# Running the last head pair with both query halves per key tile, and its batch's dispatch as one group

## The chip, the cores and the metric

The kernel runs on one core of a Trainium2 chip. The metric is device time in microseconds for one execution, lower is better. Engine names in the rows: PE is TensorE, PEld its weight loads, DVE VectorE, ACT ScalarE, POOL GpSimd, SPq the SyncE queue from which all bulk transfers are issued.

## The reference

Three blocks follow one another. First, attention with pooled queries: 4 batches, 8 heads, 1152 keys, head size 64; neighbouring queries are averaged, so there are 576 per head.

```python
q_pool = q.reshape(B, H, S // 2, 2, D).mean(axis=3)
scores = scale * np.matmul(q_pool, k.transpose(0, 1, 3, 2))
attn = softmax(scores)                      # over the 1152 keys
x = np.matmul(attn, v)                      # to (2304 tokens, 512)
```

Second, a soft mixture of 8 experts with 4 slots each (32 slots). The dispatch weights are a softmax over all 2304 tokens, so no slot input is complete before the last token is; the combine weights are a softmax over the 32 slots.

```python
logits = x @ phi                            # 2304 x 32
d = softmax(logits, axis=0); slot_input = d.T @ x
h = np.maximum(slot_input[e] @ w1[e], 0); slot_out[e] = h @ w2[e]   # per expert
c = softmax(logits, axis=1); x = c @ slot_out
```

Third, RMS norm and a gated feed-forward block with inner width 1536, which gives the output.

## The kernel before, in words

**Attention.** Heads are taken two at a time, in 16 pairs, four to a batch. Within a pair there are 9 key tiles of 128 keys and two query halves of 288 queries (`HQ`). `qk` (L421) makes the scores of one key tile and one half with eight matmuls into a two-bank PSUM tile `sc`, and ScalarE turns them into `e` (L423). `add_e` adds up the `e` tiles for the softmax sums (L438; `acc`), in two runs, key tiles 0 to 4 and 5 to 8. `av` multiplies `e` by the values (L444; four matmul instructions per key tile and half).

Pairs 1 to 14 take both halves at each key tile (9 steps, lists `STEP` and `STEP_V`); after every third key tile they do the `av` of the three. Pairs 0 and 15 are in `HALVED`: all 9 key tiles of half 0, then all 9 of half 1 (18 steps, `STEP_0`). In these two pairs VectorE shares the `acc` additions with GpSimd.

**Work beside the key loop.** `side(p)` lists what is done within pair p and when, from tables of due times (`AT`, and for some pairs `AT_0`, `AT_01`, `AT_15`); one unit of due time is one key tile of both halves. It holds the preparation of later pairs, the end of the pair before (copy of the result `take_x`, `sum_up`, `sums`, `recips`, transposes `x_turn`, division `x_divide`, logits `x_logits`, `logit_mul`, `logit_add`), and the dispatch of a finished batch (`d_turn`, `d_exp`, `d_back`, `slot_part`, `slot_turn`). Order on every engine is the order written; engines run in order.

**The last pair.** Its own end can't be put beside a next pair. In the kernel before, half 0 of pair 15 is finished while half 1 runs (the entries ending in `_a`), and batch 3 is dispatched in two groups of 288 tokens: group 3 (half 0) within the pair, group 4 (half 1) after it. `x_logits_last` makes the logits of these tokens with the tokens as the stationary side, so tokens lie on partitions, and `d_turn` turns them back with six small matmuls a group (L563). After the loop come, on the way to the slot inputs `sT`: `take_x`, `recips`, `x_logits_last(1)`, `d_turn(4)`, the exponential, `d_back`, `slot_part(4)`, `slot_copy`, and the join of the groups by the running maximum; then the first expert matmul (`hin`, L1021).

**Weights and buffers.** Each expert takes 4 MB of `w1` and `w2`, 33.6 MB for eight, and 8.4 MB of converted feed-forward weights (`away`) follow. All is loaded in this order through SyncE's queue by `load(n)`, which issues only while the program's own count of free buffers (tags `W`, `A`, `B`, `C`) allows it; at run time an issue waits until the earlier user of its buffer is done, and everything behind it on the queue waits too. `xts`, the two tiles with a batch's normalized tokens, occupy tag `W`, which is worth six units of 256 KB. In the kernel before, one is given back after group 3's `slot_part` and one after group 4's.

Of the kernel before, what the change touches and what calls it, by code (L numbers as in the profile page):

```python
# [18 lines left out]
NP = 16  # L19
# [88 lines left out]
    take_x=0.24,  # L108
    sum_up=[0.25, 0.26],
    sums=0.8,  # L110
    recips=1.33,
    inverse=[1.4, 2.41],
    x_turn=[2.3, 3.3],
    x_divide=[2.4, 3.6],
    x_logits=4.2,
    drop_x=4.25,
    logit_mul=4.8,
    logit_add=4.81,
    take_x_a=5.49,
    sums_a=5.1,  # L120
    recips_a=5.48,
    x_turn_a=[5.8, 6.1],
    x_divide_a=[5.9, 6.2],
    x_logits_a=6.15,
    d_exp_a=7.18,
    d_back_a=7.62,
    slot_part_a=8.2,
    slot_turn_a=9.43,
)
MAX_0 = [2, 1, 1, 1, 1, 0, 1, 1, 1, 1, 1, 1, 1, 1, 1, 1, 0, 0]  # L130
HALVED = (0, 15)
# [30 lines left out]
def attention_softmoe_gated_kernel(ctx: ExitStack, tc: tile.TileContext, kT, qT, vv, ip, cst, w1, w2, wg, wv, wo, rg, out):  # L162
# [311 lines left out]
    def recips(p, hs=(0, 1)):  # L474
        n = len(hs)
        q = slice(64 * hs[0], 64 * hs[-1] + 64)
        o = bank([TB, 3, 64 * n], "sumt")
        for t in range(3):
            pe.transpose(out=o[:, t, :], in_=srow[p][q, TB * t:TB * t + TB], identity=ident[q, q])
        if p == NP - 1:  # L480
            rel("B")
        if p not in rr:
            rr[p] = S([TB, 2, 3, 2], "rr")
        dv.reciprocal(rr[p][:, hs[0]:hs[-1] + 1], o.rearrange("p t (h s x) -> p h t s x", s=2, h=n)[:, :, :, :, 0])
# [52 lines left out]
    def x_logits_last(h):  # L537

        o = bank([TB, 3, 2, 32], "xl")
        if "ls" not in xl:  # L540
            xl["ls"] = S([TB, 3, 2, 2, 32], "ls", tag="lg")
        for t in range(3):
            j = 3 * h + t
            pe.matmul(o[:, t].rearrange("p s l -> p (s l)"), lhsT=xu[NP - 1][:, TB * j:TB * j + TB], rhs=ipt[:, (NP - 1) % 4, :], start=True, stop=True)
        dv.tensor_tensor(out=xl["ls"][:, :, :, h], in0=o, in1=rr[NP - 1][:, h, :, :, None].to_broadcast([TB, 3, 2, 32]), op=ALU.mult)


    dtx, dnx, psb = {}, {}, {}
    groups = [(b, (0, 1)) for b in range(3)] + [(3, (0,)), (3, (1,))]

    def d_turn(g):

        b, hs = groups[g]
        mm = S([32, 2], "mm")
        both = two_banks("lgt") if attention[0] else None
        o = []
        for i, h in enumerate(hs):
            o.append(both[0:32, i, 0:HQ] if attention[0] else bank([32, HQ], "lgt"))
            r = slice(64 * h, 64 * h + 64)
            pe.matmul(o[i], lhsT=stack[r, 0:32], rhs=lg[b][r], start=True, stop=(b < 3))  # L560
            for t in range(3 if b == 3 else 0):
                for s in range(2):
                    pe.matmul(o[i][:, TB * t:TB * t + TB], lhsT=xl["ls"][:, t, s, h], rhs=ident[0:TB, 0:TB], start=False, stop=(s == 1 and t == 2))  # L563
        if len(hs) > 1:
            dv.reduce_max(out=mm, in_=both[0:32, :, 0:HQ], axis=AX.X)
            dv.reduce_max(out=mall[:, g:g + 1], in_=mm, axis=AX.X)
        else:
            dv.reduce_max(out=mall[:, g:g + 1], in_=o[0], axis=AX.X)
        return o
# [8 lines left out]
    def d_exp(g, o, nm):  # L578
        n = len(o)
        dtx[g] = B([32, 576], F32, "dtx")  # L580
        sm = S([32, 2], "sm")
        for h in range(n):
            ac.activation(dtx[g][:, HQ * h:HQ * h + HQ], o[h], AF.Exp, bias=nm, accum_out=sm[:, h:h + 1] if n > 1 else sall[:, g:g + 1])
        if n > 1:
            dv.tensor_tensor(out=sall[:, g:g + 1], in0=sm[:, 0:1], in1=sm[:, 1:2], op=ALU.add)

    def d_back(g):
        n = 3 * len(groups[g][1])
        o = bank([TB, n, 32], "dn")
        for j in range(n):  # L590
            pe.transpose(out=o[:, j, :], in_=dtx[g][:, TB * j:TB * j + TB], identity=ident[0:32, 0:32])
# [3 lines left out]
    def d_copy(g):  # L595
        o = dpart.pop(g)
        dnx[g] = S([TB, 3 * len(groups[g][1]), 32], "dn", bufs=1, tag="ct")
        ac.copy(dnx[g], o)

    def slot_part(g):  # L600
        n, j0 = 3 * len(groups[g][1]), 3 * groups[g][1][0]
        w = 128 if n > 3 else 96
        o = bank([w, 512], "pp")
        last = n - 4 if n > 4 else 0
        for j in reversed(range(n)):
            x = xts[(j0 + j) // 3][:, (j0 + j) % 3].rearrange("p h d -> p (h d)")
            for i in range(2 if j < last else 1):
                q, c = (32 * (j + 2 * i), slice(256 * i, 256 * i + 256)) if j < last else (32 * (j % 4), slice(0, 512))
                pe.matmul(o[q:q + 32, c], lhsT=dnx[g][:, j, :], rhs=x[:, c], start=(j >= last), stop=(j < last or not last))
        dpart[g] = o, w  # L610

    def slot_copy(g, weight=None):
        o, w = dpart.pop(g)
        psb[g] = B([w, 512], F32, "psb")
        if weight is None:
            ac.copy(psb[g], o)
            if g == 3:
                rel("W")
        else:
            by = weight()  # L620
            rel("W")
# [4 lines left out]
    def slot_turn(g, to):  # L626

        w = 128 if len(groups[g][1]) > 1 else 96
        o = bank([128, 4, w], "pto")
        for k in range(4):  # L630
            pe.transpose(out=o[:, k, :], in_=psb[g][:, 128 * k:128 * k + 128], identity=ident[0:w, 0:w])
# [12 lines left out]
    def c_turn(b):  # L644
        o = bank([TB, 3, 64], "lgt")
        for t in range(3):
            pe.matmul(o[:, t], lhsT=lg[b][:, TB * t:TB * t + TB], rhs=pair.rearrange("p h l -> p (h l)"), start=True, stop=(b < 3))
            for s in range(2 if b == 3 else 0):
                pe.matmul(o[:, t], lhsT=ident[0:TB, 0:TB], rhs=xl["ls"][:, t, s].rearrange("p h l -> p (h l)"), start=False, stop=(s == 1))
# [115 lines left out]
    def side(p):  # L765
# [27 lines left out]
        if l >= 0:  # L793
# [4 lines left out]
            at("x_turn", lambda i: x_turn(l, range(3 * i, 3 * i + 3)) if p == NP - 1 else x_turn_all(l))  # L798
# [50 lines left out]
    with tc.manual_schedule():  # L849
# [64 lines left out]
        for p in range(NP):  # L914
# [3 lines left out]
            for u, (kt, h) in enumerate(steps):  # L918
# [4 lines left out]
                for i, step in enumerate(order):  # L923
# [22 lines left out]
        take_x(l, (1,))  # L946
# [3 lines left out]
        recips(l, (1,))  # L950
        load(40)
        gm = S([32, 1], "gm")
        dv.reduce_max(out=gm, in_=mall[:, 0:4], axis=AX.X)
        x_logits_last(1)
        z = bank([TB, 3, 128], "xo")
        for i in range(3):
            pe.transpose(out=z[:, i, :], in_=xu[l][:, HQ + TB * i:HQ + TB * i + TB], identity=ident)
        rel("B")
        r = rr[l][:, 1]
        for i in range(3):  # L960
            for s in range(2):
                c = slice(64 * s, 64 * s + 64)
                if i == 1:
                    dv.tensor_scalar(out=xts[1][:, i, l % 4, c], in0=z[:, i, c], scalar1=r[:, i, s:s + 1], scalar2=None, op0=ALU.mult)
                else:
                    ac.activation(xts[1][:, i, l % 4, c], z[:, i, c], AF.Copy, scale=r[:, i, s:s + 1])
# [382 lines left out]
```

## Time and profile before

| | |
|---|---|
| median of 3 runs | 748.07 us (746.56 to 752.93) |
| the profiled execution | 744.76 us, span of its instructions 742.9 us |
| pair 14 (both halves per key tile) | 424.7 to 450.9 us of the span |
| pair 15 (one half after the other) | 450.9 to 486.8 us |
| after the last `av`, up to the first expert matmul | 486.8 to 497.45 us |
| experts and the rest of the weight stream | 497.45 to about 555 us |
| feed-forward block | about 555 to 742 us |

Busy time of an engine is the union of its instructions; PE's ends are modelled, so its busy share reads high. A row of the chain gives start, duration, engine and line of one link of the work that ended last. A row of the timeline merges like instructions that follow one another on an engine. A row of stretches gives each engine's busy time (with instruction counts), the granted TensorE clock as a share of full speed, the busy share of the DMA engines and the transfer rate.

### The profile page before, as it was taken

To read this page: it belongs to the slowest core of one execution; us is meant where nothing else is said; L and a number is where in the kernel's file an instruction comes from. 1 tells how busy PE (TensorE), PEld (TensorE's weight loads), DVE (VectorE), ACT (ScalarE), POOL (GpSimd) and SP (SyncE) were. 2 spreads that over 40 slices of the span, in tenths; PEclk is the share of its full clock that TensorE was granted. 3 is DMA by queue.
4 is the path that set the end of the run, shared out by engine and by line. 5 is a ranking of instruction groups with operands and counts; after the bars stand their busy time and mean duration, and the time that the engine had idled before them with its cause. 6 is when DMAs were issued, how large, how long until landed. Compare 5 with 4: busy or idle time off the path is not lost.

```text
span 742.9 us, 15218 instructions
## 1 busy us (share of the span) xinstructions
PE 699.8 (94%) x5967; PEld 487.7 (66%) x5967; DVE 478.8 (64%) x691; ACT 391.3 (53%) x809; POOL 422.5 (57%) x340
## 2 busy tenths in 40 slices
PE   4999989899999899999999998989999999999998
PEld 2666656566666566666665665544357888888887
DVE  5968898887787887687897674432053755544420
ACT  2455656566656556565665543432155856554320
POOL 5336877876777677678777665221016854535330
PEclk9999999999999999999999999989999999999999
DMA  5221642844636617427416306079990010000001
GB/s 173 96 88 64 210 153 73 265 134 163 231 123 209 223 59 252 177 67 276 153 44 225 137 11 230 29 258 363 398 401 26 15 44 29 28 30 15 28 29 43
DMA packets 52855, 103.56 MB, mean 139 GB/s; under 512 B 5816, under 2 KB 19632, under 8 KB 52784
## 3 DMA queue, kind: packets, MB, share of 16 engines
q1 hardware_dynamic: 52784, 102.59, 39.6%
q8 instruction: 47, 0.77, 0.4%
q14 instruction: 24, 0.20, 0.1%
HBM read 89.39 MB, written 13.11 MB: 138 GB/s over the span
## 4 chain that ended last, share of the span: by engine, by line
PE 73%; DVE 13%; issue 5%; DMA 4%; ACT 3%; POOL 2%; SPq 0%; ACTq 0%; DVEq 0%; POOLq 0%
PE yo L1252 20%; PE sc L421 16%; PE av L444 15%; DVE mx L365 4%; PE mxp L364 4%; PE gv L1204 3%; DMA w<-away 2%; POOL acc L438 2%; DVE mx L371 2%; ACT e L423 2%; PE sums L469 1%; PE mxp L374 1%; PE hin L1021 1%; PE xl L521 1%; PE xo L504 1%
## 5 line engine op out<-in xcount | busy, mean ns | idle before, releaser
L438 POOL TENSOR_TENSOR acc<-acc,e 128x576 f32<-128x576 f32 x148 | 205.6, 1415 | 59.3 <-ACT e L423 49.9
L423 ACT ACTIVATE e<-sc 128x576 f32<-128x576 f32 x288 | 166.4, 657 | 93.2 <-PE sc L421 90.9
L365 DVE TENSOR_REDUCE mx<-mxp 128x2 f32<-128x1024 f32 x120 | 143.7, 1222 | 55.5 <-PE mxp L364 55.4
L444 PE MATMUL av<-e,vt 128*64 128x288 f32 x1152 | 165.2, 415 | 0.0
L438 POOL TENSOR_TENSOR acc<-e 128x576 f32<-128x576 f32 x60 | 91.9, 1549 | 95.3 <-ACT e L423 88.4
L444 PEld LDWEIGHTS av<-e,vt 128*64 128x64 f32 x1152 | 73.4, 136 | 60.5 <-issue 22.8
L421 PE MATMUL sc<-qh,kh 64*128 64x288 f32 x576 | 97.9, 329 | 3.6 <-DVE xt L513 2.8
L1252 PE MATMUL yo<-woh,hA 128*128 128x512 f32 (+1 forms) x312 | 98.9, 384 | 0.0
L421 PE MATMUL sc<-mr,pick 64*128 64x288 f32 x576 | 88.3, 294 | 1.5 <-DMA mr<-mrow 1.5
L421 PE MATMUL sc<-ql,kh 64*128 64x288 f32 x576 | 87.8, 294 | 0.0
L421 PE MATMUL sc<-qh,kl 64*128 64x288 f32 x576 | 87.7, 294 | 0.0
L1209 DVE SCALAR_TENSOR_TENSOR th<-th,gv 128x384 f32<-128x384 f32 x72 | 39.9, 554 | 62.5 <-ACT th L1206 61.9
L421 PEld LDWEIGHTS sc<-qh,kh 64*128 64x128 f32 x576 | 55.8, 185 | 28.9 <-issue 9.4
L1235 POOL TENSOR_TENSOR hA<-hu,hA 128x384 fp32r<-128x384 f32 x48 | 48.7, 1016 | 43.0 <-ACT hA L1234 39.3
L1252 PEld LDWEIGHTS yo<-woh,hA 128*128 128x128 f32 x312 | 57.6, 188 | 10.2 <-issue 0.7
L421 PEld LDWEIGHTS sc<-mr,pick 64*128 64x128 f32 x576 | 57.2, 187 | 1.9 <-DMA mr<-mrow 1.9
L1252 PE MATMUL yo<-wol,hA 128*128 128x512 f32 (+1 forms) x151 | 57.9, 383 | 0.0
L1206 ACT ACTIVATE th<-gv 128x384 f32<-128x384 f32 x72 | 35.2, 488 | 42.4 <-PE gv L1204 39.1
L421 PEld LDWEIGHTS sc<-qh,kl 64*128 64x128 f32 x576 | 57.1, 189 | 0.2
L421 PEld LDWEIGHTS sc<-ql,kh 64*128 64x128 f32 x576 | 56.9, 187 | 0.0
L364 PE MATMUL mxp<-kh,qh 64*128 64x512 f32 x240 | 49.1, 437 | 0.0
L1211 DVE SCALAR_TENSOR_TENSOR hu<-th,gv 128x384 f32<-128x384 f32 x72 | 39.9, 555 | 8.4 <-DVE th L1209 0.4
(201 smaller groups left out, 1070.9 us busy)
## 6 DMA issues: line engine op xcount, KB each, us to landing
w<-in_w_dram SPq DMA_DIRECT2D x86, 256.0 KB
w<-in_w_dram SPq DMA_DIRECT2D x21, 512.0 KB
vt<-in_vv_dram SPq DMA_DIRECT2D x16, 576.0 KB
qraw<-in_qT_dram SPq DMA_DIRECT2D x15, 576.0 KB
kraw<-in_kT_dram SPq DMA_DIRECT2D x15, 576.0 KB
away<-w SPq DMA_DIRECT2D x32, 256.0 KB
w<-away SPq DMA_DIRECT2D x32, 256.0 KB
raw<-in_wg_dram SPq DMA_DIRECT2D x12, 512.0 KB
```

The costliest lines, as they stand in the source:

```text
L364: pe.matmul(o[:, s, :], lhsT=q[r, 128 * t:128 * t + 128], rhs=k[r, 512 * c:512 * c + 512], start=True, stop=True)
L365: dv.reduce_max(out=heads[:, :, t, c], in_=o, axis=AX.X)
L421: pe.matmul(o[:, s, 0:HQ], lhsT=w[r, wk], rhs=q[r, c], start=(i == 0), stop=(i == 3))
L423: ac.activation(ets[p, kt, h], o[:, :, 0:HQ], AF.Exp, scale=0.0625)
L438: eng.tensor_tensor(out=acc[p, h, j], in0=first[p, h, j] if n == 1 else acc[p, h, j], in1=e, op=ALU.add)
L444: pe.matmul(avt[p, h][64 * s:64 * s + 64, 0:HQ], lhsT=vt[p][:, kt, 64 * s:64 * s + 64], rhs=ets[p, kt, h][:, s], start=(kt == 0), stop=(kt ...
L1204: pe.matmul(o[i], lhsT=sg[n][:, 256 * i + 128 * c:256 * i + 128 * c + 128], rhs=cT[g], start=True, stop=True)
L1206: ac.activation(t, o[0], AF.Tanh, scale=0.5)
L1209: dv.scalar_tensor_tensor(out=t, in0=t, scalar=1.0, in1=o[0], op0=ALU.add, op1=ALU.mult)
L1211: dv.scalar_tensor_tensor(out=u, in0=t, scalar=0.5, in1=o[1], op0=ALU.mult, op1=ALU.mult)
L1235: gp.tensor_tensor(out=b, in0=u, in1=f(a), op=ALU.subtract)
L1252: pe.matmul(o, lhsT=x, rhs=w[:, c], start=(ft == 0 and i == 0), stop=(ft == NF - 1 and i == 2))
```

## The change

Pair 15 leaves `HALVED` and runs like pairs 1 to 14. Pair 14's end is done at the due times of the middle pairs instead of earlier ones. Pair 15's `sums` are due at 8.55, before the last two `av` steps, and are inverted in place. After the loop the whole batch 3 is dispatched as one group of 576 tokens: logits with `ipt` (that is, phi) as the stationary side, four matmuls to bring the two heads' parts together, one exponential over both halves, six transposes back. Both `xts` tiles are given back at the end of `slot_part`. The joining of groups has four instead of five members. The PSUM pool is changed after `sT` instead of before the dispatch.

```diff
 AT_15 = dict(
-    take_x=0.24,
-    sum_up=[0.25, 0.26],
-    sums=0.8,
...
+    x_turn=5.8,
+    x_divide=[5.81, 5.82],
+    drop_x=5.83,
+    sums_a=8.55,
+    inverse_a=[8.56, 8.57],
 )
-HALVED = (0, 15)
+HALVED = (0,)
...
-        eng = dv if p in HALVED and kt % 2 == 0 else gp
+        eng = dv if p in (0, NP - 1) and kt % 2 == 0 else gp
...
+    def d_turn(b, *more):
+        mm = S([32, 2], "mm")
+        both = two_banks("lgt")
+        ins = (lg[b],) + more
+        for n, x in enumerate(ins):
+            for h in range(2):
+                r = slice(64 * h, 64 * h + 64)
+                pe.matmul(both[0:32, h, 0:HQ], lhsT=stack[r, 0:32], rhs=x[r], start=(n == 0), stop=(n == len(ins) - 1))
+        dv.reduce_max(out=mm, in_=both[0:32, :, 0:HQ], axis=AX.X)
+        dv.reduce_max(out=mall[:, b:b + 1], in_=mm, axis=AX.X)
+        return both
...
     def d_exp(g, o, nm):
-        for h in range(n):
-            ac.activation(dtx[g][:, HQ * h:HQ * h + HQ], o[h], AF.Exp, bias=nm, accum_out=sm[:, h:h + 1] if n > 1 else sall[:, g:g + 1])
+        dtx[g] = B([32, 2, HQ], F32, "dtx")
+        ac.activation(dtx[g], o[0:32, :, 0:HQ], AF.Exp, bias=nm, accum_out=sall[:, g:g + 1])
...
         if p == NP - 1:
-            at("take_x_a", lambda i: take_x(p, (0,)))
-            at("x_logits_a", lambda i: x_logits_last(0))
-            at("d_exp_a", lambda i: d_exp(3, d_turn(3), d_neg(3)))
-            at("slot_part_a", lambda i: (slot_part(3), slot_copy(3)))
...
+            at("sums_a", lambda i: sums(p))
+            at("inverse_a", lambda i: inverse(p, i))
...
         l = NP - 1
-        take_x(l, (1,))
-        phase.close()
-        recips(l, (1,))
+        take_x(l)
+        x_logits(l)
+        recips(l)
         load(40)
...
+        dv.tensor_tensor(out=z, in0=xl.pop(l), in1=srow[l], op=ALU.mult)
+        o = d_turn(3, z)
+        x_turn_all(l)
+        r = rr[l]
+        for i in range(3):
+            for s in range(2):
+                c = slice(64 * s, 64 * s + 64)
+                ac.activation(xts[0][:, i, l % 4, c], xo[l, i][0][:, i, c], AF.Copy, scale=r[:, 0, i, s:s + 1])
+        nm = S([32, 1], "nm")
+        dv.tensor_scalar(out=nm, in0=mall[:, 3:4], scalar1=gm, scalar2=-1.0, op0=ALU.max, op1=ALU.mult)
+        x_divide(l, range(3, 6))
+        d_exp(3, o, nm)
...
+        d_back(3)
+        d_copy(3)
...
+        slot_part(3)
+        slot_copy(3, weight)
         keep_b[0] = KEEP[1]
         load(40)
```

## Rows read from the trace of the kernel before

**Rows 1.** Busy time by stretch: us, PE, PEld, DVE, ACT, POOL, clock, DMA, GB/s.
```profile
424.70:450.90 26.20, 25.88 (x269) 18.17 (x267) 17.86 (x26) 12.42 (x24) 18.33 (x14) 1.00 0.23 84
450.90:486.80 35.90, 32.13 (x291) 18.97 (x290) 15.46 (x27) 14.87 (x30) 10.56 (x8) 1.00 0.35 130
486.80:497.45 10.65, 7.47 (x51) 5.00 (x52) 5.56 (x18) 3.75 (x12) 1.26 (x1) 0.86 0.77 272
497.45:510.00 12.55, 11.12 (x121) 5.63 (x122) 3.50 (x9) 3.87 (x9) 4.59 (x6) 0.85 0.91 306
510.00:555.00 45.00, 42.98 (x487) 20.98 (x487) 12.04 (x32) 14.54 (x35) 3.47 (x7) 1.00 1.05 399
555.00:742.00 187.00, 184.89 (x929) 154.62 (x927) 83.53 (x158) 94.49 (x222) 86.88 (x84) 1.00 0.09 33
```

**Rows 2.** Chain of waits, experts' stage: start, us, engine, what.
```profile
530.96 9.02 DMA w<-away
```

**Rows 3.** Chain of waits, last pair and what follows it.
```profile
453.04 2.67 DVE acc L457 x2
457.79 0.46 PE sumt L479 x3
494.15 0.27 PE sb L990 x2
497.45 2.77 PE hin L1021 x21
```

**Rows 4.** Chain of waits, pairs 12 to 14, which take both halves per key tile.
```profile
401.99 0.47 PE dn L591 x6
411.93 1.43 PE pp L609 x16
...
422.86 0.79 PE xo L504 x6
...
424.77 3.45 PE sc L421 x47
428.46 1.12 PE av L444 x8
...
430.24 0.62 PE sums L469 x8
...
437.87 0.71 PE xl L521 x4
```

**Rows 5.** Timeline, ScalarE, GpSimd and VectorE in pairs 14 and 15.
```profile
443.81 3.41 ACT L423 ACTIVATE e<-sc 128x576 f32<-128x576 f32 x6 [0.47 <-PE sc L421]
460.87 1.41 POOL L438 TENSOR_TENSOR acc<-acc,e 128x576 f32<-128x576 f32 x1 [5.79 <-ACT e L423]
467.58 0.76 DVE L438 TENSOR_TENSOR acc<-acc,e 128x576 f32<-128x576 f32 x1 [1.50 <-POOL acc L438]
```

**Rows 6.** Timeline, parts of the dispatch of batch 2 and of pairs 14 and 15.
```profile
390.33 0.68 PE L560 MATMUL lgt<-lg,cs 64*32 64x288 f32 x4
392.48 0.73 DVE L565 TENSOR_REDUCE mm<-lgt 32x2 f32<-32x576 f32 x1
...
468.26 0.45 DVE L529 TENSOR_TENSOR srow<-xl,srow 128x288 f32<-128x288 f32 x1
...
486.79 0.40 ACT L454 COPY xu<-av 128x288 f32<-128x288 f32 x1 [0.17 <-PE av L444]
489.32 0.51 ACT L966 ACTIVATE xt<-xo,rr 96x64 f32<-96x64 f32 x2 [2.13 <-PE xo L957]
```

**Rows 7.** Busy time by stretch: the part of the old last pair's time that the new one takes.
```profile
450.90:476.50 25.60, 21.83 (x205) 13.60 (x205) 11.45 (x19) 10.02 (x19) 8.44 (x7) 1.00 0.39 148
```

**Rows 8.** Timeline, SyncE's queue: issues, one row per run of like transfers.
```profile
451.46 15.75 SPq L736 DMA_DIRECT2D w<-in_w_dram  x6
483.14 4.02 SPq L731 DMA_DIRECT2D w<-in_w_dram  x4
494.25 0.38 SPq L731 DMA_DIRECT2D w<-in_w_dram  x1
```

**Rows 9.** Busy time by stretch: where the granted clock is at its lower level.
```profile
494.50:501.30 6.80, 6.13 (x44) 3.49 (x44) 2.12 (x4) 2.59 (x6) 3.31 (x3) 0.50 0.74 236
```

More of the change, by code (lines that the diff above doesn't have):

```diff
@@ L535, in logit_add @@
         rel("B")
[L537 to L545, printed above, removed]
     dtx, dnx, psb = {}, {}, {}
-    groups = [(b, (0, 1)) for b in range(3)] + [(3, (0,)), (3, (1,))]
-    def d_turn(g):
-        b, hs = groups[g]
+    def d_turn(b, *more):
         mm = S([32, 2], "mm")
[L555 to L569, printed above, removed]
+        both = two_banks("lgt")
[7 more added lines that the diff above has]
+        return both
     def d_neg(g):
@@ L578, in d_exp @@
     def d_exp(g, o, nm):
-        n = len(o)
-        dtx[g] = B([32, 576], F32, "dtx")
-        sm = S([32, 2], "sm")
-        for h in range(n):
-            ac.activation(dtx[g][:, HQ * h:HQ * h + HQ], o[h], AF.Exp, bias=nm, accum_out=sm[:, h:h + 1] if n > 1 else sall[:, g:g + 1])
-        if n > 1:
-            dv.tensor_tensor(out=sall[:, g:g + 1], in0=sm[:, 0:1], in1=sm[:, 1:2], op=ALU.add)
+        dtx[g] = B([32, 2, HQ], F32, "dtx")
+        ac.activation(dtx[g], o[0:32, :, 0:HQ], AF.Exp, bias=nm, accum_out=sall[:, g:g + 1])
     def d_back(g):
[L588 to L591, printed above, removed]
+        o = bank([TB, NBK, 32], "dn")
+        for j in range(NBK):
+            pe.transpose(out=o[:, j, :], in_=dtx[g].rearrange("p h t -> p (h t)")[:, TB * j:TB * j + TB], identity=ident[0:32, 0:32])
         rel("B")
@@ L596, in d_copy @@
         o = dpart.pop(g)
-        dnx[g] = S([TB, 3 * len(groups[g][1]), 32], "dn", bufs=1, tag="ct")
+        dnx[g] = S([TB, NBK, 32], "dn", bufs=1, tag="ct")
         ac.copy(dnx[g], o)
     def slot_part(g):
[L601 to L610, printed above, removed]
+        o = bank([128, 512], "pp")
+        for j in reversed(range(NBK)):
+            x = xts[j // 3][:, j % 3].rearrange("p h d -> p (h d)")
+            for i in range(2 if j < 2 else 1):
+                q, c = (32 * (j + 2 * i), slice(256 * i, 256 * i + 256)) if j < 2 else (32 * (j % 4), slice(0, 512))
+                pe.matmul(o[q:q + 32, c], lhsT=dnx[g][:, j, :], rhs=x[:, c], start=(j >= 2), stop=(j < 2))
+        dpart[g] = o
     def slot_copy(g, weight=None):
-        o, w = dpart.pop(g)
-        psb[g] = B([w, 512], F32, "psb")
+        o = dpart.pop(g)
+        psb[g] = B([128, 512], F32, "psb")
         if weight is None:
             ac.copy(psb[g], o)
-            if g == 3:
-                rel("W")
         else:
             by = weight()
-            rel("W")
+            rel("W", 2)
             for h in range(2):
@@ L626, in slot_turn @@
     def slot_turn(g, to):
-        w = 128 if len(groups[g][1]) > 1 else 96
-        o = bank([128, 4, w], "pto")
+        o = bank([128, 4, 128], "pto")
         for k in range(4):
-            pe.transpose(out=o[:, k, :], in_=psb[g][:, 128 * k:128 * k + 128], identity=ident[0:w, 0:w])
+            pe.transpose(out=o[:, k, :], in_=psb[g][:, 128 * k:128 * k + 128], identity=ident)
         rel("B")
@@ L646, in c_turn @@
         for t in range(3):
-            pe.matmul(o[:, t], lhsT=lg[b][:, TB * t:TB * t + TB], rhs=pair.rearrange("p h l -> p (h l)"), start=True, stop=(b < 3))
-            for s in range(2 if b == 3 else 0):
-                pe.matmul(o[:, t], lhsT=ident[0:TB, 0:TB], rhs=xl["ls"][:, t, s].rearrange("p h l -> p (h l)"), start=False, stop=(s == 1))
+            pe.matmul(o[:, t], lhsT=lg[b][:, TB * t:TB * t + TB], rhs=pair.rearrange("p h l -> p (h l)"), start=True, stop=True)
         o = o.rearrange("p t (h l) -> p h t l", h=2)
@@ L797, in side @@
             at("recips", lambda i: recips(l))
-            at("x_turn", lambda i: x_turn(l, range(3 * i, 3 * i + 3)) if p == NP - 1 else x_turn_all(l))
+            at("x_turn", lambda i: x_turn_all(l))
             at("x_divide", lambda i: x_divide(l, range(3 * i, 3 * i + 3)))
@@ L945, in attention_softmoe_gated_kernel @@
         l = NP - 1
-        take_x(l, (1,))
+        take_x(l)
+        x_logits(l)
+        recips(l)
+        load(40)
+        gm = S([32, 1], "gm")
+        dv.reduce_max(out=gm, in_=mall[:, 0:3], axis=AX.X)
+        z = B([128, HQ], F32, "z")
+        dv.tensor_tensor(out=z, in0=xl.pop(l), in1=srow[l], op=ALU.mult)
+        rel("B")
+        o = d_turn(3, z)
[5 more added lines that the diff above has]
+                ac.activation(xts[0][:, i, l % 4, c], xo[l, i][0][:, i, c], AF.Copy, scale=r[:, 0, i, s:s + 1])
@@ new lines, in attention_softmoe_gated_kernel @@
+        dv.tensor_scalar(out=st, in0=st, scalar1=sall[:, 3:4], scalar2=1e-9, op0=ALU.add, op1=ALU.add)
+        dv.reciprocal(st, st)
+        dv.tensor_scalar(out=al, in0=al, scalar1=st, scalar2=None, op0=ALU.mult)
+        ad = B([32, 3, 32], F32, "ad")
+        dv.tensor_tensor(out=ad, in0=ident[0:32, None, 0:32].to_broadcast([32, 3, 32]),
+                         in1=al[:, :, None].to_broadcast([32, 3, 32]), op=ALU.mult)
+        dv.tensor_tensor(out=lg[3], in0=lg[3], in1=z, op=ALU.add)
+        rel("B")
@@ new lines, in weight @@
+        def weight():
+            o = bank([128, 1], "sb")
+            pe.matmul(o, lhsT=stack[0:32, :], rhs=st, start=True, stop=True)
+            wt = S([128, 1], "wt", bufs=1)
+            dv.tensor_copy(wt, o)
+            return wt
+        slot_part(3)
+        slot_copy(3, weight)
+        keep_b[0] = KEEP[1]
+        load(40)
+        o = bank([128, 3, 32], "br")
+        pe.matmul(o.rearrange("p b s -> p (b s)"), lhsT=ones2, rhs=ad.rearrange("p b s -> p (b s)"), start=True, stop=True)
@@ new lines, in attention_softmoe_gated_kernel @@
+        rel("B")
+        sT = S([128, 4, 32], "sT", bufs=1)
+        p3 = pt[:, 0:3]
+        dv.tensor_tensor(out=p3, in0=p3, in1=o[:, :, None, :].to_broadcast([128, 3, 4, 32]), op=ALU.mult)
+        dv.tensor_reduce(out=sT, in_=p3.rearrange("p b k s -> p k s b"), axis=AX.X, op=ALU.add)
+        o = bank([128, 4, 32], "pto")
+        for k in range(4):
+            pe.matmul(o[:, k, :], lhsT=psb[3][:, 128 * k:128 * k + 128], rhs=stack[:, 0:32], start=True, stop=True)
+        rel("B")
+        dv.tensor_tensor(out=sT, in0=sT, in1=o, op=ALU.add)
@@ L949, in attention_softmoe_gated_kernel @@
         ps = phase.enter_context(tc.tile_pool(name="ps2", bufs=1, space=PSUM))
-        recips(l, (1,))
[L951 to L966, printed above, removed]
@@ L982, in attention_softmoe_gated_kernel @@
-        dv.reciprocal(st, st)
-        dv.tensor_scalar(out=al, in0=al, scalar1=st, scalar2=None, op0=ALU.mult)
-        ad = B([32, 4, 32], F32, "ad")
-        dv.tensor_tensor(out=ad, in0=ident[0:32, None, 0:32].to_broadcast([32, 4, 32]),
-                         in1=al[:, :, None].to_broadcast([32, 4, 32]), op=ALU.mult)
-        def weight():
-            o = bank([TB, 1], "sb")
-            pe.matmul(o, lhsT=stack[0:32, 0:TB], rhs=st, start=True, stop=True)
-            wt = S([TB, 1], "wt", bufs=1)
-            dv.tensor_copy(wt, o)
-            return wt
@@ L995, in attention_softmoe_gated_kernel @@
-        slot_part(4)
-        slot_copy(4, weight)
-        keep_b[0] = KEEP[1]
-        load(40)
-        o = bank([128, 4, 32], "br")
-        pe.matmul(o.rearrange("p b s -> p (b s)"), lhsT=ones2, rhs=ad.rearrange("p b s -> p (b s)"), start=True, stop=True)
-        rel("B")
-        sT = S([128, 4, 32], "sT", bufs=1)
-        dv.tensor_tensor(out=pt, in0=pt, in1=o[:, :, None, :].to_broadcast([128, 4, 4, 32]), op=ALU.mult)
-        dv.tensor_reduce(out=sT, in_=pt.rearrange("p b k s -> p k s b"), axis=AX.X, op=ALU.add)
@@ L1005, in attention_softmoe_gated_kernel @@
-        o = bank([128, 4, 32], "pto")
-        for k in range(4):
-            pe.matmul(o[:, k, :], lhsT=psb[4][:, 128 * k:128 * k + 128], rhs=stack[0:TB, 0:32], start=True, stop=True)
-        rel("B")
-        dv.tensor_tensor(out=sT, in0=sT, in1=o, op=ALU.add)
         so = accum("so")
```

54 lines of the change are left out of this document (12 added, 42 removed).

## The prediction, on record before the result was known

> **What bounds the kernel now.** I read the stretches first [rows 1], because the busy shares of the whole span mix stages with different limits. There the reader sees four regimes. In pair 14 TensorE is busy 25.88 of 26.20 us. In pair 15 it is still the busy engine, 32.13 of 35.90 us, but the same 18 score and 18 `av` blocks take 9.7 us more than in pair 14, although pair 14 also makes maxima for a later pair. From 510 to 555 the transfers run at 399 GB/s with a DMA share of 1.05, and from 555 on TensorE has 184.89 of 187.00 us. The chain of waits says the same of the experts' stage: there it follows transfers, 9.02 us in one piece [rows 2]. So the end of the kernel is the end of the weight stream plus a feed-forward block that the change doesn't touch; what the change is worth is by how much the stream ends sooner. The stream waits for buffers: SyncE's queue had its last attention-time loads out by 467.2 us and next issued at 483.14, when a tile of tag `W` came back, and at 494.25, when the second did [rows 8]. An earlier end of the pair and of the dispatch therefore moves it, if nothing else holds the queue.
>
> **Pair 15, part by part.** Both forms start at 450.9, the code ahead being the same. In the middle form three key tiles cost six score blocks, 3.45 us, and three times two `av`, 1.12 us each [rows 4]: 3.45 + 3.36 = 6.81 us.
> - Key tiles 0 to 2: pair 14's `sums` now stand at 2.75, after the first `av`, that is at 450.9 + 3.45 + 1.12 = 455.5. VectorE's two additions for it end at 453.04 + 2.67 = 455.7 [rows 3], so TensorE still waits 0.2 us; then sums 0.62 [rows 4] and their transposes 0.46 [rows 3]. Together 8.1 us, to 459.0. In the kernel before, the same wait came right after the second score block and held TensorE until 455.7; it is mostly covered now by score blocks and `av`.
> - Key tiles 3 to 5: logits 0.71 and transposes 0.79 of pair 14 [rows 4]: 8.3 us, to 467.3.
> - Key tiles 6 to 8: the new `sums` stand ahead of the last two `av` and wait for the last `acc` addition. What is queued behind this wait is two `av`, so it counts. From this stretch's start the six exponentials run from 0.85 to 4.26 us at 0.57 each [rows 5], as in pair 14, whose scores began at 442.96. Key tile 7 is ready at 0.85 + 3 x 0.57 = 2.56, GpSimd adds its halves in 2 x 1.41, to 5.38, and VectorE the last of tile 8 in 0.76 [rows 5], to 6.14. TensorE comes to the second run of sums at 3.45 + 1.12 + 0.62 = 5.19, waits 0.95, does them in 0.62 and the last `av` in 2.24: 9.05 us with one hop. The last `av` ends at 476.4, call it 476.5, against 486.8: **10.3 us earlier**.
>
> Removed with that are half 0's own dispatch inside the pair, and the doubled small steps; they are in pair 15's 32.13 us. Added copies, divisions and sums on VectorE and GpSimd lie beside TensorE: VectorE has 15.46 us of work in the old pair's 35.90 and GpSimd 10.56 [rows 1]. If that cover failed, the place to see it would be the sums' wait just costed.
>
> **The dispatch after it.** From the last `av`: copy of the last half 0.40 [rows 6]; logits 0.71 [rows 4]; transposes of the sums 0.46 [rows 3]; small VectorE steps about 0.3 and the multiplication 0.45 [rows 6]; head sums 0.68 [rows 6]; five hops between engines about 0.25. That is 3.25 us. Then ScalarE has six scaled copies ahead of the exponential, 3 x 0.51 [rows 6], which begin after half of the 0.79 us of transposes [rows 4]: 1.9 us, longer than the maxima beside them (0.73 [rows 6] and some 0.4 for the small ones). The exponential over both halves costs what a score block's does, 0.6, and 0.2 for its sum; then six transposes 0.47 [rows 4], a copy 0.35, `slot_part` 1.43 [rows 4], and from there the old path, 497.45 - 494.15 = 3.30 us [rows 3]. The sum is 3.25 + 1.9 + 0.8 + 0.47 + 0.35 + 1.43 + 3.30 = 11.5 us against 10.65 [rows 1]. An exponential over this shape and a wide one-group end aren't in the trace; the nearest rows put them between 0.5 and 1.1 us, so the whole lies between 10.7 and 14. The first expert matmul comes at 476.5 + 11.5 = 488.0, **9.4 us earlier**.
>
> **The stream.** Bytes by rate and time [rows 1]: 130 GB/s over 35.9 us, 272 over 10.65, 306 over 12.55 and 399 over 45 make 4.67 + 2.90 + 3.84 + 17.96 = 29.4 MB. From 486.8 to 555 are 24.7 MB, 61.9 us at full rate, in 68.2 us: 6.3 us of it are lost to waits for buffers. By 476.5 some 148 x 25.6 = 3.8 MB had been moved [rows 7], by issues that end before either form's first half is done with its buffers. If the new kernel has moved as much by its last `av`, 25.6 MB are left, 64.1 us: the stream ends at 476.5 + 64.1 + 6.3 = 546.9, 8.1 us earlier, and 12.4 earlier if only 2 us are lost. Both tiles of `W` now return together, some 8.3 us after the last `av`, at 484.8: that is 1.7 us later than the first and 9.5 earlier than the second did [rows 8]. At 476.5 the buffers of keys, values and the `e` tiles come free, some 3 MB and about 8 us of transfers, which just reach to 484.8. Between 8.1 and 12.4 I take **9 us**, nearest to the 9.4 of the first expert matmul, since what is lost to buffers follows the experts.
>
> On SyncE's queue nothing else is moved. A load due within pair 15 goes only into a counted-free buffer, and the six `e` tiles alive in the middle form leave at least as many free at 5.84 and 6 as were used before.
>
> **A rule against the change.** The rows show TensorE, not its neighbours, full beside half 0's dispatch [rows 1]. The Trainium skill (Perfetto Trace Analysis, Optimizing Scalar/DVE Operations) says that where Scalar or Vector cause bubbles on other engines, smaller instructions may let work finish sooner, which is what two groups do. By it, the first group's cover would be worth a whole dispatch, and the sum would be about zero; by the row it is worth 0.9 us.
>
> **Rivals.**
> - *The dispatch is exposed.* All of batch 3's chain now lies after the key loop, and if its steps add instead of widen, it takes twice 10.65, 21.3 us, and the experts start at 476.5 + 21.3 = 497.8: no change, 748. For it: TensorE has only 7.47 us of work in the old 10.65. Against: the wider forms in the middle pairs [rows 4, 6] are far under twice the narrow ones. Chance 0.15.
> - *The clock falls sooner.* The granted clock was 0.50, the 1.2 GHz level, from 494.5 to 501.3 [rows 9], after the thin stretch in which TensorE was busy 7.47 of 10.65 us; before it, in full work, it was at the upper level. If it falls early in the new dispatch, up to half of the roughly 5 us of matmuls in it are added again and the first expert runs slow for longer: 4 to 5 us of the 9 are lost, 743.5. The Trainium skill (TensorE: Matmul & The Clock Gate, The HAM clock gate) says that the throttled clock is the default and activity releases it; by that a longer thin stretch is a risk. Rows 9 agree in direction. Chance 0.13.
> - *The queue is held.* A load in pair 15 draws a buffer that only the dispatch gives back; in the old pair one such wait already held the queue for most of 15.75 us [rows 8]. Everything behind it then starts at about 485, with the 3.8 MB of pair 15 still to move: 29.4 MB at 399 GB/s are 73.6 us, less some 1 MB moved before, 71.1, plus 6.3: 562.4 instead of 555, slower by 7.4 to 8, about 756. It decides if the held issue stands before about 465. Against: `W` isn't counted free before `slot_part`, and the count gives `e` buffers back early. Chance 0.10.
>
> **How the numbers follow.** The forecast, 7 to 12 us gained, has the remaining 0.62. The terms are sums of one profiled execution of 744.76 us, which is 3.3 below the median of 748.07 and under the lowest of the three; it would become 735.8, and the median, moved alike, 739.1. I predict 739. Its own range is 735 to 742. The likeliest rivals on the same side and at zero reach to 749.5, so 735 to 749.5 leaves out the held queue and the far ends. A measurement of this kernel tells about 1%, 7.5 us, from no change. Of the forecast's 0.62 about 0.50 is beyond 7.5 us and 0.12 within; the clock and the exposed dispatch are within (0.28); with a little of the queue's case within, that gives 0.50 faster, 0.39 same, 0.11 slower.
>
> **What would show it.** Right: the last `av` near 476.5, the first expert matmul near 488, all three visits of pair 15 at 8 to 9 us, issues on SyncE's queue resuming by 477, and the first `yo` matmul of the feed-forward block some 9 us earlier. Wrong: a wait at the new `sums` of over 3 us, a dispatch over 15 us, a lower clock before 484, a gap on SyncE's queue from before 465 to 485, or a stream that ends at 555 although the experts start early.

## The result, and the profile after

The changed kernel takes 738.28 us in the median of 4 runs (737.26 to 738.66), the kernel before 750.12 us in the median of its 4 (746.56 to 752.93). The ratio is 0.9868, 95% interval 0.9833 to 0.9902: 1.3% faster, some 10 us by the ratio and 11.8 between the medians. On two other chips it was 0.981 (0.9773 to 0.9846) and 0.9842 (0.9805 to 0.9879). The two traces differ by less, 744.76 to 738.22 us, because the execution traced of before was one of its fastest; the runs of before scatter by 6.4 to 9.3 us on a chip, those of the changed kernel by 1.4 to 5.2.

Busy time by stretch of the changed kernel, columns as in [rows 1]: pair 15, the dispatch, the first experts, the weight stream, the feed-forward block.

```profile
450.06:475.81 25.75, 24.00 (x253) 15.95 (x253) 16.89 (x23) 11.95 (x24) 11.04 (x8) 1.00 0.46 168
475.81:488.56 12.75, 9.62 (x56) 5.22 (x56) 5.68 (x19) 4.24 (x14) 1.26 (x1) 0.78 0.62 208
488.56:500.00 11.44, 10.12 (x104) 4.91 (x108) 3.49 (x9) 3.86 (x9) 4.58 (x6) 0.80 0.91 304
...
510.00:548.50 38.50, 35.77 (x378) 17.19 (x378) 11.07 (x28) 12.27 (x29) 2.90 (x5) 1.00 1.04 385
548.50:735.00 186.50, 184.57 (x928) 154.53 (x926) 83.23 (x158) 94.32 (x222) 86.88 (x84) 1.00 0.09 34
...
475.81:483.01 7.20, 4.62 (x31) 2.08 (x35) 3.58 (x14) 2.90 (x11) 0.00 (x0) 1.00 0.65 218
...
483.01:493.25 10.24, 9.69 (x66) 5.56 (x58) 2.10 (x6) 2.87 (x6) 3.75 (x3) 0.50 0.78 268
```

The last two rows are the stretches just before and at the lower clock. Pair 15 takes 25.75 us where it took 35.90 [rows 1], the dispatch 12.75 where it took 10.65, and the last block, cut where the weight stream ends, is unchanged within 0.5 us. The chain of waits through pair 15 and the dispatch (start, us, engine, what):

```profile
454.87 0.62 PE sums L453 x8
...
472.22 0.76 DVE acc L422
...
473.02 0.69 PE sums L453 x8
...
480.25 0.71 ACT xt L904 x3
480.97 0.69 ACT dtx L547 x2
...
481.70 0.48 PE dn L552 x6
...
482.57 2.42 PE pp L567 x16
485.00 0.53 PE sb L931 x2
...
488.56 3.64 PE hin L966 x32
```

Pair 14's sums no longer follow a wait, as they did behind 453.04 in [rows 3]; the new sums wait for the last addition (472.22), and `slot_part` (pp) takes 2.42 us against 1.43 in [rows 4]. SyncE's queue (start, us, issues):

```profile
469.30 6.88 SPq L684 DMA_DIRECT2D w<-in_w_dram  x3
476.27 1.80 SPq L689 DMA_DIRECT2D w<-in_w_dram  x4
484.16 1.29 SPq L684 DMA_DIRECT2D w<-in_w_dram  x2
485.51 28.23 SPq L689 DMA_DIRECT2D w<-in_w_dram  x38
```

After its loads of the pair's first part the queue goes on at 469.30 and 476.27; in the kernel before it went on only at 483.14 [rows 8]. It then waits until 484.16, when `W` comes back in the course of `slot_part`. The clock (0.50 in the first fence's last row) is at its lower level for 10.2 us instead of 6.8 [rows 9], and falls at 483.01, 0.4 us after `slot_part` began; in the kernel before it fell at 494.5, behind `slot_part`.

Executions start pair 15 at different times, since short stretches at the lower clock lie in the first pairs of some. So I count from pair 15's first exponential, in us (`away` are the last weights of the stream, `yo` is of the feed-forward block):

| trace | start of pair 15 | last `av` | first expert matmul | first `away` issue | first `yo` matmul |
|---|---|---|---|---|---|
| before | 451.8 | 34.9 | 45.6 | 79.2 | 102.8 |
| before, second trace | 456.7 | 35.0 | 45.4 | 79.2 | 102.3 |
| changed | 450.9 | 24.9 | 37.6 | 73.7 | 96.9 |
| changed, second and third | 448.5, 448.9 | 24.9, 24.9 | 37.5, 37.8 | 73.0, 73.4 | 96.3, 96.7 |

From pair 15 on the change gains 5.4 to 6.5 us. Some 3 us more lie ahead of it: pairs 5, 9 and 13 take 30.4, 30.5 and 30.4 us from first exponential to first exponential in the kernel before, and 29.3, 29.3 and 29.7 in the changed one. Together that is 8 to 9.5 us.

### The profile page after: what moved, and what is told of

Read it like the earlier page. It is cut to its first block, busy times and chain, and to the rows that moved or that the text cites. A ratio compares the mean times of both kernels' runs of the same rounds, so it can differ in the third digit from the quotient of the medians.

```text
span 736.4 us, 15111 instructions
## 1 busy us (share of the span) xinstructions
PE 696.9 (95%) x5924; PEld 486.1 (66%) x5924; DVE 479.6 (65%) x684; ACT 388.5 (53%) x800; POOL 424.0 (58%) x340
## 4 chain that ended last, share of the span: by engine, by line
PE 71%; DVE 11%; DMA 7%; issue 4%; ACT 3%; POOL 2%; SPq 0%; ACTq 0%; DVEq 0%; POOLq 0%
PE yo L1197 20%; PE sc L405 17%; PE av L428 15%; DVE mx L349 4%; DMA w<-in_w_dram 4%; PE mxp L348 3%; PE gv L1149 3%; ACT e L407 2%; DMA w<-away 2%; POOL acc L422 2%; DVE mx L355 2%; PE xo L490 1%; PE xl L507 1%; PE mxp L358 1%; PE sums L453 1%
## 5 line engine op out<-in xcount | busy, mean ns | idle before, releaser
L422 POOL TENSOR_TENSOR acc<-e 128x576 f32<-128x576 f32 x60 | 93.4, 1574 | 90.8 <-ACT e L407 83.7
L405 PE MATMUL sc<-qh,kh 64*128 64x288 f32 x576 | 95.1, 326 | 0.8 <-DVE mx L349 0.6
L405 PE MATMUL sc<-mr,pick 64*128 64x288 f32 x576 | 86.8, 296 | 1.5 <-DMA mr<-mrow 1.5
L405 PE MATMUL sc<-qh,kl 64*128 64x288 f32 x576 | 86.2, 295 | 0.0
L405 PE MATMUL sc<-ql,kh 64*128 64x288 f32 x576 | 86.1, 294 | 0.0
L1197 PEld LDWEIGHTS yo<-woh,hA 128*128 128x128 f32 x312 | 57.6, 188 | 10.2 <-issue 0.7
L405 PEld LDWEIGHTS sc<-mr,pick 64*128 64x128 f32 x576 | 55.4, 187 | 2.0 <-DMA mr<-mrow 2.0
L405 PEld LDWEIGHTS sc<-qh,kl 64*128 64x128 f32 x576 | 55.6, 189 | 0.3
L405 PEld LDWEIGHTS sc<-ql,kh 64*128 64x128 f32 x576 | 55.2, 188 | 0.0
```

The source lines that it names most:

```text
L405: pe.matmul(o[:, s, 0:HQ], lhsT=w[r, wk], rhs=q[r, c], start=(i == 0), stop=(i == 3))
L1197: pe.matmul(o, lhsT=x, rhs=w[:, c], start=(ft == 0 and i == 0), stop=(ft == NF - 1 and i == 2))
```

## The experiments

Three sets, each on one chip with its own runs of the kernel before; "changed" is the changed kernel's median on the same chip where it ran there.

| run | median us (runs) | before | ratio, 95% interval | changed |
|---|---|---|---|---|
| a0_changed_again | 736.07 (6) | 751.78 | 0.981 (0.9773 to 0.9846) | |
| x1_later_sums | 743.96 (6) | 751.78 | 0.9904 (0.9871 to 0.9937) | 736.07 |
| x2_halves_kept | 740.04 (6) | 751.78 | 0.9842 (0.9805 to 0.988) | 736.07 |
| x3_delay | 743.36 (6) | 751.78 | 0.99 (0.9866 to 0.9934) | 736.07 |
| b1_before_again | 749.3 (1) | 747.83 | | |
| x4_early_sums | 739.06 (6) | 747.83 | 0.9869 (0.9834 to 0.9905) | |
| i1_fill | 734.49 (6) | 747.83 | 0.9807 (0.9767 to 0.9847) | |
| i2_shorter | 734.33 (6) | 747.83 | 0.9818 (0.978 to 0.9856) | |
| a1_changed_third | 736.28 (6) | 748.73 | 0.9842 (0.9805 to 0.9879) | |
| x5_two_exps | 739.51 (6) | 748.73 | 0.9879 (0.9841 to 0.9918) | 736.28 |
| x6_one_exp | 743.45 (12) | 748.73 | 0.9938 (0.9909 to 0.9967) | 736.28 |
| i3_fill_and_shorter | 732.45 (6) | 748.73 | 0.9794 (0.9761 to 0.9826) | 736.28 |

**The changed kernel again (a0, a1).** No edit.

> The changed kernel once more, as the measure for the others of this set on the same chip. Its first trace is 6.5 us shorter than the one of before (744.76 to 738.22), the medians differ by 10 to 12. If the traces tell the gain, 6 to 7 us here; if the kernel before is often slower than its trace, 9 to 12, and then its runs scatter by several us while these stay within 1.5.

It was the second case, and more: 15.7 us. The runs of before, 744.05 to 753.3, go roughly with their mean granted clock: 0.993 at 744.05 and 0.979 to 0.989 in the others. These runs scatter too, by 5.2 us.

> The changed kernel again, as the measure on this chip for the three beside it: 736 to 739 us, pair 15's first exponential to the first yo matmul 96 to 97 us.

As expected: 736.28 us, and 96.7 from pair 15 to `yo`.

**Pair 14's sums later, in the kernel before (x1).**

```diff
-    sums=0.8,
-    recips=1.33,
-    inverse=[1.4, 2.41],
+    sums=1.6,
+    recips=1.75,
+    inverse=[1.8, 2.41],
```

> The kernel before with pair 14's sums due at 1.6 instead of 0.8, its reciprocals at 1.75 and 1.8: the wait for the acc additions is then beside score and av blocks. If the gain comes from that wait (idle 2.9 us at the sums in the trace of before), the experts start 2 to 3 us earlier and the time falls by 2 to 3 us. If the pair's length is the doubled small steps and half 0's dispatch alone, it falls by under 1 us, since TensorE only waits elsewhere.

TensorE's waits in pair 15 of the kernel before, us in total, times, longest, have this row, and the variant has none with sums:

```profile
PE sums L469 <- DVE acc L457: 2.9, 2, 1.7
```

The last `av` comes 32.5 us after pair 15's first exponential instead of 34.9, and `yo` 99.4 instead of 102.8. So the wait is worth 2.4 us in the pair and about 3 at the end, as the theory said for the traces. The runs fell by 7.8 us, well over the 2 to 3 expected and more than the trace explains; see the open point.

**Halves one after the other, in the changed kernel (x2).**

```diff
-HALVED = (0,)
+HALVED = (0, 15)
...
-    sums_a=8.55,
-    inverse_a=[8.56, 8.57],
+    sums_a=8.75,
+    inverse_a=[8.76, 8.77],
```

> The changed kernel, but pair 15 again does half 0 for all key tiles and then half 1; the dispatch stays one group, and pair 14's end stays at the later due times. My theory: TensorE has the same blocks in either order, so it is the dispatch in one group and the covered wait that shorten the pair; last av some 28 us after the pair's start against 25.7, experts 2 to 3 us later than in the changed kernel, time 2 to 3 us above it. Rival, both halves per key tile is the gain: the last av stays at 34 us or more and the time at that of the kernel before.

Stretches of pair 15 and of the dispatch, columns as above:

```profile
451.10:479.54 28.44, 26.18 (x254) 16.34 (x253) 15.17 (x23) 12.15 (x23) 10.90 (x8) 0.95 0.39 144
479.54:492.34 12.80, 9.68 (x55) 5.04 (x54) 5.30 (x18) 4.25 (x14) 1.26 (x1) 0.77 0.61 209
```

The pair takes 28.4 us, 2.7 more than the changed one and 7.5 less than before; the dispatch is as in the changed kernel, `yo` comes 2.2 to 2.8 us later, and the runs are 4.0 us longer. Part of the pair's 2.7 is a stretch at the lower clock (mean 0.95). Taking both halves per key tile is thus the smaller part: some 2.9 of the 10 us at the last `av`, and 2.2 to 2.8 of the 5.4 to 6.5 at `yo`. The dispatch in one group and the covered wait, which x2 keeps together, are the larger.

**A delay ahead of the exponential, in the changed kernel (x3).** Ten copies that nothing uses:

```diff
+        scr = B([128, 576], F32, "scr")
+        for i in range(10):
+            ac.copy(scr, xu[l])
+        rel("B")
         d_exp(3, o, nm)
```

> The changed kernel with ten more copies on ScalarE (about 0.6 us each, 6 us in all) ahead of the dispatch's exponential; they compute nothing that is used. If the end hangs on the dispatch through the buffers it gives back, the time grows by 5 to 6.5 us over the changed kernel. If the weight stream would end at the same time anyway, by under 2 us.

The ten copies in the list of groups (busy us, mean ns), SyncE's longest wait, and the clock:

```profile
L911 ACT COPY scr<-xu 128x576 f32<-128x576 f32 x10 | 6.7, 672 | 0.3
```

```profile
SPq L684 <- PE pp L567: 10.6, 2, 10.1
```

```profile
480.60:497.60 17.00, 10.19 (x67) 5.38 (x68) 3.07 (x11) 8.56 (x17) 3.17 (x3) 0.50 0.39 144
```

6.7 us of delay move the first expert matmul by 7.3 to 7.7 us and the time by 7.3. The queue waits for `slot_part`, which gives `W` back, and the clock is low for 17 us. The end hangs on the dispatch; the rival is out. The delay moves both the return of `W` and the first experts, so x3 does not tell which of the two counts.

**The kernel before, a second trace (b1).** No edit.

> The kernel before once more, for a trace of its common case: its runs lie mostly at 750 to 753 us with a mean granted clock of 0.98, while the trace read for the prediction has 744.76 and 0.993, and the variant with the later sums ran at 742 to 745. Theory: the wait at pair 14's sums lets the clock fall in pair 15 in most executions, so the trace shows a lower-level stretch that begins between 455 and 480 us, and pair 15 at 40 us or more instead of 35. Rival: the low stretches lie in the first pairs and pair 15 takes 35 us as before.

Stretches of this trace: a low one near the start, one in pair 7, and pair 15.

```profile
53.20:56.60 3.40, 3.40 (x30) 3.27 (x30) 1.71 (x2) 1.84 (x4) 1.70 (x2) 0.50 1.04 392
...
254.60:258.00 3.40, 3.40 (x16) 1.54 (x14) 3.40 (x6) 0.40 (x1) 1.85 (x2) 0.50 1.01 314
455.80:491.60 35.80, 32.03 (x290) 18.86 (x289) 15.46 (x27) 14.88 (x29) 10.50 (x8) 1.00 0.35 130
```

For this execution the theory fell: pair 15 runs at the upper level and takes what it took before. Its mean clock, 0.989, is not that of the slowest executions (0.979 to 0.982), of which there is no trace. Pair 15 starts 4.9 us later than in the first trace, which has only the low stretch near the start; here 107.8 to 111.2 and the one in pair 7 are added.

**Pair 14's sums early, in the changed kernel (x4).**

```diff
 AT_15 = dict(
+    sum_up=[0.25, 0.26],
+    sums=0.8,
+    recips=1.33,
+    inverse=[1.4, 2.41],
```

> The changed kernel with pair 14's sums, reciprocals and inversions at the due times of the kernel before (0.8, 1.33, 1.4, 2.41); loop and dispatch stay. Theory: TensorE again waits about 3 us for the acc additions and the clock falls in part of the executions: 3 to 8 us above the changed kernel, with a mean clock under that of the changed kernel in most runs. Rival, the wait costs only itself: 2 to 3.5 us above, the clock as in the changed kernel.

TensorE's waits in its pair 15; the first row is the new sums' wait, the second pair 14's:

```profile
PE sums L457 <- DVE acc L426: 1.8, 1, 1.8
PE sums L457 <- DVE acc L445: 1.7, 1, 1.7
```

The last `av` comes 27.0 us after the first exponential instead of 24.9, `yo` 97.7 instead of 96.3 to 96.9, and the mean clock of its runs, 0.988 to 0.995, is that of the changed kernel. The rival holds in the pair, where the wait costs 2.1 us; at the end it is nearer to 1, because the dispatch is shorter in this trace, 12.0 us against 12.6 to 13.0. The changed kernel did not run on this chip, so its runs give no finer figure.

**Batches 0 to 2 (x5, x6).** Counting the pairs showed a part of the change that the prediction had passed over: `d_exp` is also the dispatch of the three earlier batches. In the kernel before it ends with a VectorE addition of two sums. Timeline of the kernel before where pair 13 begins (in brackets: idle before, releaser):

```profile
394.75 0.65 DVE L585 TENSOR_TENSOR sall<-sm 32x1 f32<-32x1 f32 x1 [1.19 <-ACT dtx L583]
395.33 1.00 DVE L513 TENSOR_TENSOR xt<-xo,rr 96x384 f32<-96x384 f32 x2
...
396.48 0.40 PE L421 MATMUL sc<-qh,kh 64*128 64x288 f32 x2 [0.91 <-DVE xt L513]
```

The same in the changed kernel, where one exponential sums both halves:

```profile
393.54 1.00 DVE L499 TENSOR_TENSOR xt<-xo,rr 96x384 f32<-96x384 f32 x2
393.70 0.73 ACT L547 ACTIVATE dtx<-lgt,nm 32x576 f32<-32x576 f32 x1 [3.24 <-DVE nm L540]
```

Behind the addition the division of x comes 1.8 us later, and the next score block waits 0.91 us for the PSUM tile that it frees. x5 puts the addition back into the changed kernel, x6 takes it out of the kernel before (the mirror image):

```diff
...
+        sm = S([32, 2], "sm")
+        for h in range(2):
+            ac.activation(dtx[g][:, h], o[0:32, h, 0:HQ], AF.Exp, bias=nm, accum_out=sm[:, h:h + 1])
+        dv.tensor_tensor(out=sall[:, g:g + 1], in0=sm[:, 0:1], in1=sm[:, 1:2], op=ALU.add)
```

> The changed kernel, but batches 0 to 2 have their dispatch's exponential as in the kernel before: one for each half, and a VectorE addition of the two sums. Theory: that addition waits for ScalarE on VectorE's queue, the division of x behind it comes late, and the next score block waits for its PSUM buffer, 1.1 us in each of pairs 5, 9 and 13: those pairs 30.4 us long again instead of 29.3, time 3 to 3.5 us above the changed kernel, nothing else moved. Rival, the pairs differ by chance and clock: under 1 us.

```profile
398.02 0.66 DVE L553 TENSOR_TENSOR sall<-sm 32x1 f32<-32x1 f32 x1 [1.19 <-ACT dtx L552]
398.62 1.00 DVE L499 TENSOR_TENSOR xt<-xo,rr 96x384 f32<-96x384 f32 x2
...
399.77 0.40 PE L405 MATMUL sc<-qh,kh 64*128 64x288 f32 x2 [0.92 <-DVE xt L499]
```

The wait is back, the pairs take 30.5 us each, 2.7 to 3.1 us more in all, and the median is 3.2 us above the changed kernel. That nothing else moved was wrong. Pair 15 and the last dispatch are the changed kernel's own code, but in this trace the clock fell only behind `slot_part`:

```profile
486.77 1.50 PE pp L573 x16
...
488.50:495.30 6.80, 6.18 (x44) 3.62 (x43) 1.59 (x4) 2.48 (x5) 3.12 (x3) 0.50 0.95 341
```

The first expert matmul came 11.6 us after the last `av` instead of 12.6 to 13.0, and `yo` 93.5 us after pair 15's start instead of 96.3 to 96.9. So the same code reached `yo` some 3 us sooner in the trace whose clock fell 1.1 to 1.5 us later, and for 6.8 us instead of 10.2. The runs scatter by 6.7 us, so the agreement of 3.2 with the pairs' sum is closer than they can show.

> The kernel before, with one exponential over both halves and no addition for batches 0 to 2; pair 15 and the last dispatch as before. Theory: pairs 5, 9 and 13 at 29.3 us, 3 to 3.5 us under the kernel before, the stretch from pair 15's first exponential to the first yo matmul at 102 to 103 us as before. Rival: under 1 us.

Without it the pairs of the kernel before take 29.7, 29.3 and 29.7 us, the stretch from pair 15 to `yo` stays at 102.5, and the time falls by 5.3 us, 0.6% (interval 0.3 to 0.9%). The pairs give 2.6 of that in the traces, and pairs 4 and 12 another 0.5. The last `av` and the first expert matmul come 1.0 to 1.2 us earlier after pair 15's start than in the kernel before, and yet `yo` does not: not every gain ahead of the experts reaches the end.

**Improvements (i1, i2, i3).** i1 fills the dispatch's gaps on TensorE with matmuls that nothing uses; i2 moves the new sums behind one more `av` and leaves all divisions to VectorE:

```diff
+        busy = accum("busy")
+        for i in range(4):
+            pe.matmul(busy[:, 0:256], lhsT=ident, rhs=cs, start=True, stop=True)
...
         d_back(3)
+        for i in range(1):
+            pe.matmul(busy[:, 0:256], lhsT=ident, rhs=cs, start=True, stop=True)
```

> The changed kernel with five extra matmuls of 256 columns in the dispatch's gaps (four after the transposes, one after the transposes back); their result is not used. In the changed kernel the clock was at its lower level from 483.0 to 493.3 and slot_part took 2.42 us there against 1.43. If idle gaps ahead of it lower the clock, it now stays up: slot_part 1.4 to 1.5, experts 1.5 to 2.5 us earlier after the last av, time 1.5 to 3 us under the changed kernel. If the clock falls anyway: no gain, or 0.5 us lost.

The chain of waits of i1 behind the transposes back:

```profile
482.34 0.63 PE busy L917 x2
482.96 1.43 PE pp L567 x16
...
486.92 1.49 PE hin L971 x9
```

`slot_part` is at 1.43 us again, the experts start 10.9 us after the last `av` instead of 12.6 to 13.0, `yo` comes 93.5 us after pair 15's start instead of 96.3 to 96.9. The clock falls only at 486.7, 10.8 us after the last `av`. In the eight traces of the one-group dispatch without fillers it falls 6.9 to 8.5 us after it, and in i3, which has fillers too, at 10.6. x5 came as far at `yo` without them, so how much of the 2.8 to 3.4 us at `yo` the fillers give in every execution is not shown.

```diff
-    sums_a=8.55,
+    sums_a=8.85,
...
-                ac.activation(xts[0][:, i, l % 4, c], xo[l, i][0][:, i, c], AF.Copy, scale=r[:, 0, i, s:s + 1])
...
+        x_divide(l, range(0, 3))
```

> The changed kernel with pair 15's sums one av later (due 8.85) and with both halves' divisions on VectorE instead of six scaled copies on ScalarE ahead of the exponential. TensorE's wait at these sums was 1.75 us in the trace of the changed kernel and shrinks to about 0.6; the exponential starts 0.8 us earlier. Last av 1 us and experts 1.5 to 2 us earlier, time 1.5 to 2 us under the changed kernel. If the stream alone sets the end: under 0.5 us.

The new sums' wait in i2:

```profile
PE sums L453 <- DVE acc L422: 0.8, 1, 0.8
```

The last `av` comes 1.0 us and the first expert matmul 2.0 to 2.4 us earlier, `yo` 2.6 to 3.2. The changed kernel did not run on the chip of i1 and i2, and their ratios to the kernel before overlap with a0's, so their gain in time is read from the traces alone. Both at once:

> The changed kernel with both improvements: the sums one av later, all divisions on VectorE, and four filling matmuls (three and one). Each alone shortened the stretch from pair 15 to the first yo matmul by 2.7 to 3.3 us in its trace. If they add: 4.5 to 5.5 us under the changed kernel; if both only spare the same clock loss: 3 to 3.5 us.

```profile
449.20:473.76 24.56, 23.77 (x253) 15.71 (x251) 15.90 (x22) 11.77 (x23) 10.79 (x8) 1.00 0.47 169
473.76:484.25 10.49, 9.40 (x64) 5.17 (x64) 7.03 (x21) 3.07 (x8) 0.57 (x1) 1.00 0.61 198
```

732.45 us, 3.8 below the changed kernel on that chip; it is the fastest of all. They add only in part: the pair's 1 us does, the dispatch is at 10.5 us against 10.9 and 11.6 alone.

## Why the prediction was right, and where it was not

The time was right, 738.28 against 739, and so were the direction and the pair. That the number came out so near is partly luck: the gain from pair 15 on was 5.4 to 6.5 us instead of 9, and some 3 us came from an edit that the sum had left out.

- *Pair 15.* Predicted 25.6 us, measured 25.75. The three visits took 8.1, 7.9 and 9.7 us, against 8.1, 8.3 and 9.05 in the sum. The third was longer because the wait at the new sums was 1.75 us, not 0.95. The sum counted one VectorE addition of 0.76 us behind GpSimd's; there are two, and the first held the second back to 472.22. Timeline of GpSimd and VectorE there, two additions in each row:

```profile
468.75 2.93 POOL L422 TENSOR_TENSOR acc<-acc,e 128x576 f32<-128x576 f32 x2 [6.20 <-ACT e L407]
470.35 2.62 DVE L422 TENSOR_TENSOR acc<-acc,e 128x576 f32<-128x576 f32 x2 [1.31 <-POOL acc L422]
```

- *The dispatch.* Predicted 11.5 us, measured 12.75. The step that failed is `slot_part` and what follows, taken at upper-level durations: 2.42 us instead of 1.43, and 0.53 instead of 0.27 behind it. The rival "the clock falls sooner" was in part what happened, and its sign, a lower clock before 484, came true at 483.01. i1 and x5 show it, since where the clock falls later, `slot_part` takes 1.43 and 1.50. The Trainium skill (TensorE: Matmul & The Clock Gate, The HAM clock gate) says that the throttled clock is the default and that how busy the engine has been sets it. In direction the trace agrees: TensorE had been busy 4.62 of the 7.20 us up to 483.01, its longest wait in them 2.1 us.
- *The stream.* The step that failed is "9 us": the first expert matmul came 7.6 to 8.2 us earlier after pair 15's start, but the stream's later issues only 5.5 to 6.2. The sum kept the loss to waits for buffers at 6.3 us, on the ground that buffers freed at the last `av` would carry some 3 MB up to the return of `W`. `W` came back at 484.16, as good as forecast (484.8), but up to 483.01 only 218 GB/s over 7.20 us, 1.6 MB, had been moved. From 475.81 on the changed trace moves 208 x 12.75, 304 x 11.44, some 390 x 10 and 385 x 38.5, 24.9 MB: 62.3 us at 399 GB/s, in 72.7 us, so 10.4 are lost, over half of it in the dispatch. The clock has a part in it: in x5 and i1, where it fell later, `yo` came 93.5 us after pair 15's start, 8.8 to 9.3 before that of the kernel before, which is the gain that was predicted.
- *What was missing.* The one-exponential edit of `d_exp` for batches 0 to 2, 0.7 to 1.2 us in each of three pairs, which x5 and x6 show in both directions. The prediction costed it for batch 3 alone.
- *The rule against the change* (smaller instructions to let work finish sooner) did not decide: the dispatch grew by 2.1 us, of which some 1.2 are the lower clock, not by 10.65.
- *Left open.* The runs of before lie mostly at 747 to 753 us, with mean clocks of 0.979 to 0.989, the changed kernel's at 734 to 740, with 0.988 to 0.993. Traces explain 8 to 9.5 us of the 12 to 16 between the medians; the rest goes with that clock, by no experiment. The low stretch in pair 7 is in b1, x1 and x5, all with two exponentials, and in none of the ten traces with one; the first trace of before has two exponentials and lacks it. x1, whose edit lies in pair 15 alone, ran at 0.988 to 0.993 beside a kernel before that ran at 0.979 to 0.989 but once, which points to the wait at pair 14's sums. But x4, which puts these sums back early in the changed kernel, stayed at 0.988 to 0.995. What lowers the clock in the slowest executions, and where, no trace shows.

## What to carry to other kernels

Follow an edited helper to all its callers: a one-column addition that waits on another engine's queue cost some 3 us over three earlier batches that the change's name doesn't mention. Where a stream of weights sets the end, count how much it can move until its buffers are returned, not only when the work behind them begins. And a tail written as one chain can thin TensorE's work until the granted clock falls, so cost its durations at both levels, or fill the gaps.

## What the runs showed of the hardware that was not expected

With five filling matmuls in 2.5 us of gaps (four in i3) the granted clock fell 10.6 to 10.8 us after the last `av`, behind `slot_part`, instead of 6.9 to 8.5, and in i1 the first expert matmul came 1.6 to 2.0 us nearer to the last `av`, although they stand on the same queue as the work. The same dispatch code without them lost its upper clock at different points in different executions, 7.0 to 8.5 us after the last `av` in four traces (the changed kernel's three and x5), and `yo` moved by some 3 us with it. One VectorE addition of 128x576 took 1.9 us while a GpSimd addition ran, and 0.76 us behind it; that the one slows the other was not tested. The kernel before started its last pair 4.9 us apart in two executions; two more short stretches at the lower clock in the pairs ahead account for some 3.3 of that.
